# Rounding four weight pieces and preparing chunk 4 ahead of the first join, in an RWKV-7 plus squared-ReLU kernel

## The chip, the cores and the metric

The kernel runs on one core of one Trainium2 chip. The time is the device time of one execution in microseconds (us); the figure given for a kernel is the median of its runs. The core has five engines, each with its own instruction stream, worked off in order: TensorE (PE, matrix products and transposes), VectorE (DVE), ScalarE (ACT), GpSimd (POOL) and SyncE (SP, which here only issues DMAs). An instruction that has to wait holds up everything behind it on its engine.

## The reference

The first half is a recurrence over 768 tokens for 4 batches of 8 heads with head size 40; the second half is a dense layer pair with a squared ReLU on the result, seen as 3072 tokens of 320 numbers.

```python
for t in range(S):
    y[:, :, t] = np.einsum('bhd,bhde->bhe', rt, state)
    Sa = np.einsum('bhde,bhe->bhd', state, at)
    state_decay = state * wt[:, :, None, :] - np.einsum('bhd,bhe->bhde', Sa, bt)
    state = state_decay + np.einsum('bhd,bhe->bhde', vt, kt)
x = y.transpose(0, 2, 1, 3).reshape(B * S, H * D)
h = np.maximum(x @ w_in, 0.0)          # w_in 320 x 2048, w_out 2048 x 320
out = (h * h @ w_out).astype(np.float32)
```

The two weight matrices arrive as 64-bit floats. The kernel reads them as pairs of 32-bit words and makes 32-bit floats of them itself.

## The kernel before

**Chunks and slots.** The tokens are cut into 24 chunks of 128 (6 per batch, the four batches in turn: chunk 0 to 3 are the first of each batch). After a prologue the main loop (L968) runs one *slot* per chunk. Slot i finishes chunk i (`chain`, L604: its first result on ACT is `xr`, L619), makes the parts of chunk i+1 that need no state (`rest` in the first four slots, `sorted_slot` later), and makes `early` parts of later chunks. The dictionary `ahead` says of which: slot 0 makes those of chunks 4 and 5, slot 1 of 6 and 7, slot 2 of 8 and 9, slot 3 of 10, slot 4 of 11 and 12, slot 5 of 13 and 14, and each later slot one.

**The early part of a chunk** (`early`, L342) loads w, b and a (three 160 KB loads on SP), transposes them on PE (L316, three groups of 4), makes running products and reciprocals on DVE (L352, L353, L357, L358, L364, L365), multiplies two of them on PE (L371, listed as L87 `ps_w<-decay,bT`), and copies the result on ACT into the tile `N` (L373 to L377). There is one `N` buffer. From `N` SP stores pieces to DRAM (`kept_q`, `kept_m`, `kept_n`, later `kept_d`), and it stores the decays (`kept_e`). The copy into `N` for the next chunk waits until all stores of the last one have landed. Both `N` and the four PSUM buffers `ps_w` are shared by what the slot does besides.

**Solves and joins.** The triangular systems of a *unit* of chunks (units 0 and 1 are one chunk each, then two chunks each up to chunk 11, then four) are solved on POOL (`solve`, L422 to L453): it fetches `kept_q` into `half_n` (L420), runs 31 pairs of L448 and L450, and stores `kept_t`. The `join` of a chunk (`inverses`, L457) loads `kept_t` as `blocks` (L470), transposes it on DVE (L482) and combines it on PE and ACT (L484, L494, L501) into `T`, which `chain` multiplies with (`xr,T`). Chunk 0's join can't begin before unit 0 is solved.

**Weights.** 26 pieces have to be rounded (`rounding`, L251), two generator steps each; a piece's last instructions come in the next piece's first step. A piece is two ACT instructions (L258, L262) and five DVE ones (L275, L276, L277, L266, L267), with two PSUM buffers `ps_f`. Pieces 0 to 9 (w_in and w_third) are 512 wide, 10 to 25 (w_out) 320 wide. The raw words are fetched in 1 MB fetches (0 to 4, in four or five DMAs) into `wide` buffers and then in 320 KB fetches; `then` (L237) issues a fetch on SP when a piece that held its buffer is done. Fetch 0 is issued by POOL in step 8 of the solve of unit 1, fetch 1 by SP after chunk 0's join, fetch 2 by POOL in step 4 of the solve of unit 2. Slots 0 to 3 round 4, 6, 6 and 7 pieces (`pieces_in`), slot 4 the rest (`halves`).

**The dense layers** (`Ffn`, L689) are woven into the slots from slot 4 on. `thirds` and `whole` need the first ten pieces, `make_quarter` all 26. What is left of them after the last slot runs in `rest` (L760).

The order on each engine is written out: `go`, `run` and `weave` step the generators, `later` and `tick` delay stores and fetches by a step or two.

Of the kernel before, what the change touches and what calls it, by code (L numbers as in the profile page):

```python
# [17 lines left out]
def kernel(  # L18
# [22 lines left out]
    nc = tc.nc  # L41
    ctx.enter_context(tc.manual_schedule())
    B, H, S, D = r.shape
# [72 lines left out]
    class Ring:  # L116
# [6 lines left out]
        def next(self):  # L123
            self.at = (self.at + 1) % len(self.tiles)
            return self.tiles[self.at]
# [10 lines left out]
    order = [(bb, c) for c in range(NCH) for bb in range(B)]  # L136
# [205 lines left out]
    def early(i, g=None, apart=False):  # L342

        x_ = early_loaded.pop(i)
        dec = decays.next() if g is None else kept_here[i]
        if g is not None:
            nc.vector.memset(dec[:, :A_, :, MID:MID + 1], 1.0)
        up, down, aT = (dec[:, n] for n in (UP, DOWN, A_))
        wT = turn(x_["w"])
        yield  # L350
        for q in range(NP):
            nc.vector.tensor_tensor_scan(up[:, q, MID + 1:C + 1], wT[:, q, MID:], ones, 1.0, Alu.mult, Alu.mult)  # L352
            nc.vector.tensor_tensor_scan(down[:, q, MID - 1::-1], wT[:, q, MID - 1::-1], ones, 1.0, Alu.mult, Alu.mult)  # L353
        yield
        if not apart:
            bT_, aT_ = turn(x_["b"]), turn(x_["a"])
        nc.vector.reciprocal(down[:, :, MID + 1:C + 1], up[:, :, MID + 1:C + 1])  # L357
        nc.vector.reciprocal(up[:, :, :MID], down[:, :, :MID])  # L358
        yield
        if apart:  # L360
            bT_, aT_ = turn(x_["b"]), turn(x_["a"])
            yield
        bT = turned("bT", 1)
        nc.vector.tensor_tensor(bT, bT_, down[:, :, 1:C + 1], Alu.mult)  # L364
        nc.vector.tensor_tensor(aT[:, :, :C], aT_, up[:, :, :C], Alu.mult)  # L365
        if g is None:
            store(kept_e[i], dec[:USED])
        yield
        bb, c = order[i]
        t_ = new("N", [128, H, C], 1)  # L370
        for e, p_ in enumerate(products(bT, aT[:, :, :C])):  # L371
            plain, flip_ = t_[:, e:NP:2], t_[:, NP + e::2]
            nc.scalar.copy(plain, p_[:, ::2])  # L373
            for half in range(2):
                own_, other = (slice(n * HC, (n + 1) * HC) for n in (half, 1 - half))
                nc.scalar.copy(flip_[own_, :, own_], p_[other, 1::2, other])  # L376
            nc.scalar.copy(flip_[:HC, :, HC:], p_[:HC, 1::2, HC:])  # L377
        joins = lambda half: t_[half * HC:half * HC + Q, :, half * HC + Q:(half + 1) * HC]
        for half in range(2):
            for n in range(2):  # L380
                at = half * HC + n * Q
                if i < SMALL:
                    kept, to = kept_q[i, :, half, n], at + Q
                else:
                    u = unit_of[i]
                    kept, to = kept_d[u][i - units[u][0], :, half], (half + 1) * HC
                    kept = kept[:, n * Q * HC:n * Q * HC + Q * (to - at)].rearrange("h (s t) -> h s t", s=Q)
                store(kept.rearrange("h s t -> s h t"), t_[at:at + Q, :, at:to], 1, nc.scalar if g is not None and n else nc.sync)
            if i < SMALL and g is None:
                store(kept_m[i][half], joins(half), 1)  # L390
        if g is None:
            store(kept_n[i], t_[:HC, :, HC:], 1)
        else:
            g["dec"], g["N"] = dec, new("N21", [HC, H, HC], 2)
            nc.scalar.copy(g["N"], t_[:HC, :, HC:])
            g["joins"] = spare("joins", i)
            for half in range(2):
                nc.scalar.copy(g["joins"][half * HC:half * HC + Q], joins(half))
        yield
# [11 lines left out]
    def take(u, queues, words=slice(None)):  # L411
        first, nb = units[u]
        if u < FINE:
            kept = kept_q[first:first + nb].rearrange("b h f k s t -> (b h f k) (s t)")
        else:
            kept = kept_d[u].rearrange("b h f w -> (b h f) w")
        cols = classes(u)
        rows = 128 // cols
        for col in range(cols):
            queues[col % len(queues)].dma_start(out=part_of(u)[col * rows:(col + 1) * rows, words], in_=kept[:, words])  # L420

    def solve(u, between={}):  # L422
        run(solving(u, between))
# [177 lines left out]
    halves = (slice(0, HC), slice(HC, C))  # L601
# [170 lines left out]
    second = Ffn()  # L772
# [3 lines left out]
    def run(gen):  # L776
        for _ in gen:
            tick()
# [13 lines left out]
    def prepare(i, g=None, apart=False, steps=0):  # L792
        gen = early(i, g, apart)
        for _ in range(steps):
            next(gen)
            yield
        if i + 1 < len(order) and i + 1 not in early_loaded:
            load_early(i + 1)
        yield from gen
# [6 lines left out]
    ready = {0: {}, 1: {}}  # L806
    own = [nc.gpsimd]
# [5 lines left out]
    def go(gen, n=1):  # L813
        for _ in range(n):
            next(gen, None)
            tick()

    weights = moe_w_in.dtype != FP32
    rounded = rounding() if weights else as_they_are()

    def weights_by(n, queue):
        if weights:
            fetch_weights(n, queue)

    e0, e1, e2, e3 = (early(i, ready[i]) if i in ready else prepare(i) for i in range(B))
    r0, first_slot = rest(0, ready[0]), chain(0, ready[0])
    go(e0, 3)
    go(e1)  # L830
# [25 lines left out]
    flush()  # L856
    join = inverses(0, ready[0])
    go(join)
    go(e3)
    flush()  # L860
    solve(1, {8: lambda: weights_by(0, nc.gpsimd), 20: lambda: take(2, own)})
    run(r0)
    run(join)
    weights_by(1, nc.sync)
    solve(2, {4: lambda: weights_by(2, nc.gpsimd)})
    for gen in (e0, e1, e2, e3):
        run(gen)
    flush()
    tc.no_sync_barrier()


    TOTAL = 12
    ahead = {0: (4, 5), 1: (6, 7), 2: (8, 9), 3: (10,), 4: (11, 12), 5: (13, 14)}
    ahead.update({i: (i + 9,) for i in range(6, len(order) - 9)})

    pieces_in = {0: (4, TOTAL), 1: (6, TOTAL), 2: (6, TOTAL), 3: (7, TOTAL)}
    done = set(range(B))
    unit = unit_of[B]


# [27 lines left out]
    def sorted_slot(i, g, ch):  # L908
        j = i + 1
        more = j < len(order)  # L910
        n = ready.setdefault(j, {}) if more else None
        made = [prepare(m_, apart=True, steps=4 * at) for at, m_ in enumerate(ahead.get(i, ()))]
        one, two = (made + [iter(()), iter(())])[:2]
        early_join = more and "joining" in n
        joining = n.pop("joining") if early_join else inverses(j, n) if more else iter(())
        fine = more and unit_of[j] < FINE

        def step(*what):
            for w_ in what:
                w_()  # L920
            tick()

        of = lambda fn: (lambda: fn(j, n)) if more else (lambda: None)
        on = lambda gen: lambda: next(gen, None)
        begun = i > B

        def extra():
            if not begun:
                second.thirds()
                second.whole()  # L930

        halves = lambda: [next(rounded, None) for _ in range(2)] if not begun else None

        if more:
            begin(j, n)
        step(second.make_quarter, halves, halves)
        step(of(turn_rv), on(one), on(one), halves)
        fetch_next(j + 1, "r")
        step(second.make_quarter, halves)
        step(on(ch), of(decay_state))  # L940
        step(of(make_rv), second.thirds)
        step(on(ch), on(one), on(two), on(two))
        if fine:
            next(joining, None)
        step(second.whole, on(two))
        step(on(ch), extra)
        step(on(one), of(turn_k))
        step(on(one), on(ch), of(turn_down))
        step(on(ch), of(scale_kb))
        if fine:  # L950
            next(joining, None)
        step(on(ch), of(make_a), second.thirds, on(one))
        fetch_next(j + 1, "v")
        step(of(turn_state), second.square, second.whole, on(two), on(two))
        if not early_join:
            next(joining, None)
        step(extra)
        run(ch)
        if more:
            n["chain"] = chain(j, n)  # L960
            next(n["chain"])
        loads(j + 1)
        step(second.square, second.make_quarter)
        step(second.make_quarter, on(two))
        for gen in (one, two, joining):
            run(gen)
# [53 lines left out]
```

## Time and profile before

| | us |
|---|---|
| median of 3 runs | 990.28 (987.42 to 990.52) |
| the profiled execution | 987.0 |
| its span, first to last instruction | 985.3 |
| PE busy in the span | 875.7 (89%) |
| DVE, ACT, POOL busy | 485.0, 275.5, 576.1 |
| `xr` (L619) of chunks 1, 2, 3, 4, 5 | 106.8, 156.1, 204.3, 243.4, 291.8 |

The page gives the busy time of each engine, the span in 40 slices of 24.6 us with the busy share in tenths, the clock that TensorE was granted, and the chain of work that ended last. The timeline gives instructions in order of time: start, duration, engine, line, operation, output and inputs, how many were merged, and in brackets how long the engine had stood idle before and what ended that. "SPq" rows are DMA issues. The `xr` times mark the slots: between the one of chunk i and the one of chunk i+1 lies slot i.

### The profile page before, as it was taken

To read this page: it belongs to the slowest core of one execution; us is meant where nothing else is said; L and a number is where in the kernel's file an instruction comes from. 1 tells how busy PE (TensorE), PEld (TensorE's weight loads), DVE (VectorE), ACT (ScalarE), POOL (GpSimd) and SP (SyncE) were. 2 spreads that over 40 slices of the span, in tenths; PEclk is the share of its full clock that TensorE was granted. 3 is DMA by queue.
4 is the path that set the end of the run, shared out by engine and by line. 5 is a ranking of instruction groups with operands and counts; after the bars stand their busy time and mean duration, and the time that the engine had idled before them with its cause. 6 is when DMAs were issued, how large, how long until landed. Compare 5 with 4: busy or idle time off the path is not lost.

```text
span 985.3 us, 21632 instructions
## 1 busy us (share of the span) xinstructions
PE 875.7 (89%) x8752; PEld 725.8 (74%) x8752; DVE 485.0 (49%) x868; ACT 275.5 (28%) x711; POOL 576.1 (58%) x989
## 2 busy tenths in 40 slices
PE   6447666667897999999999999999999999999998
PEld 4436555556685888888888888888888888887776
DVE  5528775758755454475446655632444423331111
ACT  3132423234323342332223232322222222222111
POOL 4788482836018985999976999959999800000000
PEclk9757565657698999999999999999999999999999
DMA  8987987894667579465588772585404364030000
GB/s 100 143 160 131 191 158 164 171 170 118 91 127 132 100 138 183 92 122 78 97 167 156 124 113 70 102 183 82 66 19 78 82 121 71 14 64 8 14 13 14
DMA packets 263431, 104.16 MB, mean 106 GB/s; under 512 B 246148, under 2 KB 252676, under 8 KB 261924
## 3 DMA queue, kind: packets, MB, share of 16 engines
q1 hardware_dynamic: 259188, 86.39, 50.9%
q0 software_dynamic: 3056, 16.26, 6.9%
q8 instruction: 69, 1.13, 0.5%
q10 hardware_dynamic: 1088, 0.13, 0.1%
q14 instruction: 30, 0.25, 0.1%
HBM read 70.11 MB, written 30.66 MB: 102 GB/s over the span
## 4 chain that ended last, share of the span: by engine, by line
PE 64%; SPq 1%; DVE 1%; DMA 1%; ACT 0%; issue 0%; ACTq 0%
PE ps_f L87 36%; PE ps_w L87 11%; PE ps_c L87 11%; PE ps_w L316 4%; PE ps_c L560 1%; PE ps_c L643 1%; PE ps_w L544 1%; DMA dec<-kept_e 1%; SPq L108 1%; SPq L464 0%; DMA tokens<-tokens 0%; DVE decay L357 0%; DVE state L535 0%; DVE RV L332 0%; ACT N L376 0%
## 5 line engine op out<-in xcount | busy, mean ns | idle before, releaser
L448 POOL TENSOR_TENSOR half_p<-half_n,half_t 128x120 f32<-128x120 f32 (+37 forms) x438 | 255.7, 584 | 84.4 <-DMA half_n<-kept_d 26.5
L450 POOL TENSOR_TENSOR half_t<-half_t,half_p 128x120 f32<-128x120 f32 (+37 forms) x438 | 275.9, 630 | 34.3
L87 PE MATMUL ps_f<-w_out,hid 128*128 128x320 f32 x768 | 217.4, 436 | 0.0
L87 PEld LDWEIGHTS ps_f<-w_out,hid 128*128 128x128 f32 x768 | 142.5, 190 | 54.6 <-issue 0.2
L87 PE MATMUL ps_f<-tokens,w_in 128*128 128x256 f32 x672 | 157.2, 388 | 0.0
L87 PEld LDWEIGHTS ps_f<-tokens,w_in 128*128 128x128 f32 x672 | 126.7, 194 | 17.9 <-issue 1.0
L734 DVE TENSOR_TENSOR hid<-hid 128x512 f32<-128x512 f32 x96 | 88.9, 963 | 50.2 <-ACT hid L727 49.7
L727 ACT ACTIVATE hid<-ps_f 128x512 f32<-128x512 f32 x84 | 50.2, 597 | 96.0 <-PE ps_f L87 96.0
L352 DVE TENSOR_TENSOR_SCAN decay<-ps_w,ones 128x64 f32<-128x64 f32 x88 | 23.8, 271 | 81.5 <-PE ps_w L316 81.5
L669 DVE TENSOR_TENSOR tokens<-ps_c,dec 128x512 f32<-128x512 f32 x24 | 16.5, 688 | 79.3 <-PE ps_c L87 79.3
L87 PE MATMUL ps_w<-decay,bT 40*128 40x128 f32 x352 | 30.0, 308 | 27.0 <-DVE decay L365 27.0
L373 ACT COPY N<-ps_w 128x256 f32<-128x256 f32 x48 | 17.7, 369 | 121.6 <-PE ps_w L87 74.7
L87 PEld LDWEIGHTS ps_w<-decay,bT 40*128 40x128 f32 x352 | 27.6, 213 | 30.2 <-issue 19.1
L510 DVE TENSOR_TENSOR kvT<-ps_w,dec 128x512 f32<-128x512 f32 x24 | 16.5, 688 | 66.9 <-ACT minus_x L630 33.9
L87 PE MATMUL ps_f<-tokens,w_third 64*128 64x256 f32 x336 | 46.9, 385 | 1.5 <-DVE w_out L266 1.5
L332 DVE TENSOR_TENSOR RX<-ps_w,upper 128x512 f32<-128x512 f32 x48 | 30.8, 683 | 32.1 <-PE ps_w L87 31.6
L332 DVE TENSOR_TENSOR RV<-ps_w,upper 128x512 f32<-128x512 f32 x48 | 30.9, 686 | 31.1 <-PE ps_w L87 30.8
L87 PEld LDWEIGHTS ps_c<-xr,T 64*64 64x64 f32 x768 | 30.7, 149 | 20.5 <-issue 15.0
L522 ACT COPY rT<-ps_w 128x512 f32<-128x512 f32 x24 | 14.0, 585 | 108.3 <-PE ps_w L316 108.3
L87 PE MATMUL ps_c<-xr,T 64*64 64x40 f32 x768 | 36.8, 243 | 3.6 <-ACT xr L619 1.6
L357 DVE RECIPROCAL decay<-decay 128x256 f32<-128x256 f32 x22 | 38.2, 1736 | 0.0
L532 DVE TENSOR_TENSOR f<-end,dec 128x4 f32<-128x4 f32 x20 | 5.1, 255 | 66.6 <-DMA dec<-kept_e 66.6
(130 smaller groups left out, 1411.7 us busy)
## 6 DMA issues: line engine op xcount, KB each, us to landing
kept_e<-decay SPq DMA_DIRECT2D x22, 633.8 KB
dec<-kept_e SPq DMA_DIRECT2D x22, 633.8 KB
hid<-in_moe_w_out_dram SPq DMA_DIRECT2D x16, 320.0 KB
half_n<-kept_d POOLq DMA_DIRECT2D x6, 768.0 KB, 10.3
in_w<-in_w_dram SPq DMA_DIRECT2D x24, 160.0 KB
in_ab<-in_b_dram SPq DMA_DIRECT2D x24, 160.0 KB
in_ab<-in_a_dram SPq DMA_DIRECT2D x24, 160.0 KB
in_k<-in_k_dram SPq DMA_DIRECT2D x24, 160.0 KB
```

The lines of the kernel that those rows point to most:

```text
L87: nc.tensor.matmul(o, l_, r_, start=start, stop=True, skip_group_check=True)
L316: nc.tensor.transpose(p_[:, q * 128:(q + 1) * 128], pair(x_, q), ident)
L332: nc.vector.tensor_tensor(t_, p_, over4(upper), Alu.mult)
L352: nc.vector.tensor_tensor_scan(up[:, q, MID + 1:C + 1], wT[:, q, MID:], ones, 1.0, Alu.mult, Alu.mult)
L357: nc.vector.reciprocal(down[:, :, MID + 1:C + 1], up[:, :, MID + 1:C + 1])
L373: nc.scalar.copy(plain, p_[:, ::2])
L448: nc.gpsimd.tensor_tensor(p_, part[:, at:at + m_].unsqueeze(1).to_broadcast([128, n, m_]), t3[:, :n, s:s + 1].to_broadcast([128, n, m_]), ...
L450: nc.gpsimd.tensor_tensor(t3[:, :n, s + 1:], t3[:, :n, s + 1:], p_, Alu.subtract)
L510: nc.vector.tensor_tensor(kT, kT_, down[:, :, 1:C + 1], Alu.mult)
L669: nc.vector.tensor_tensor(t_, y_, g["up"][:, :, :C], Alu.mult)
L727: nc.scalar.activation(h_, p_.rearrange("p f t -> p (f t)"), Act.Relu)
L734: nc.vector.tensor_tensor(h_, h_, h_, Alu.mult)
```

## The change

Fetches 0 and 1 are issued by SP right after the first eight loads. Four pieces are rounded, and chunk 4's early part is begun (four of its five steps), between the DMA issue of chunk 0's join and the rest of that join. Fetch 2 takes fetch 0's place in the solve of unit 1, and the solve of unit 2 issues none. Slots 0 to 3 now round 5, 6, 6 and 6 pieces, slot 4 none; and the early parts are made one chunk further on: slot 0 makes chunk 5's alone, slot 3 those of 10 and 11, slot 4 of 12 and 13, slot 5 chunk 14's alone.

```diff
+    weights_by(0, nc.sync)
+    weights_by(1, nc.sync)
-    e0, e1, e2, e3 = (early(i, ready[i]) if i in ready else prepare(i) for i in range(B))
+    e0, e1, e2, e3, e4 = (early(i, ready[i]) if i in ready else prepare(i) for i in range(B + 1))
...
     join = inverses(0, ready[0])
     go(join)
+    go(rounded, 2 * 4)
     go(e3)
     flush()
-    solve(1, {8: lambda: weights_by(0, nc.gpsimd), 20: lambda: take(2, own)})
+    go(e4, 4)
+    solve(1, {8: lambda: weights_by(2, nc.gpsimd), 20: lambda: take(2, own)})
     run(r0)
     run(join)
-    weights_by(1, nc.sync)
-    solve(2, {4: lambda: weights_by(2, nc.gpsimd)})
-    for gen in (e0, e1, e2, e3):
+    solve(2)
+    for gen in (e0, e1, e2, e3, e4):
         run(gen)
...
-    ahead = {0: (4, 5), 1: (6, 7), 2: (8, 9), 3: (10,), 4: (11, 12), 5: (13, 14)}
-    ahead.update({i: (i + 9,) for i in range(6, len(order) - 9)})
+    ahead = {0: (5,), 1: (6, 7), 2: (8, 9), 3: (10, 11), 4: (12, 13)}
+    ahead.update({i: (i + 9,) for i in range(5, len(order) - 9)})
-    pieces_in = {0: (4, TOTAL), 1: (6, TOTAL), 2: (6, TOTAL), 3: (7, TOTAL)}
-    done = set(range(B))
+    pieces_in = {0: (5, TOTAL), 1: (6, TOTAL), 2: (6, TOTAL), 3: (6, TOTAL)}
+    done = set(range(B + 1))
...
-        halves = lambda: [next(rounded, None) for _ in range(2)] if not begun else None
...
-        step(second.make_quarter, halves, halves)
-        step(of(turn_rv), on(one), on(one), halves)
+        step(second.make_quarter)
+        step(of(turn_rv), on(one), on(one))
         fetch_next(j + 1, "r")
-        step(second.make_quarter, halves)
+        step(second.make_quarter)
```

In the order of instructions that the changed program has, SP issues the eight DMAs of fetches 0 and 1 ahead of chunk 0's first `kept_q` stores. On SP the join's `blocks` load is followed by fetch 3 (five DMAs) and one 320 KB fetch, and only then come the stores of chunk 3's `N`. On PE the products of chunk 4 (`decay,bT`) stand between chunk 0's join and its first `xr,T`; on ACT the copies into `N` for chunk 4 stand between the join's L501 and the chain's first L630.

## The prediction

> **What bounds the kernel now.** I read the slices of the page first: they say when TensorE is the bound.
>
> ```profile
> PE   6447666667897999999999999999999999999998
> PEclk9757565657698999999999999999999999999999
> DMA  8987987894667579465588772585404364030000
> ```
>
> From about 325 us on PE is full at full clock; before 260 us it is half busy at a clock of 0.5 to 0.7 while the DMA engines are near full. So the end is the moment at which PE saturates plus a fixed amount of PE work. A microsecond counts if it moves that moment, or adds to or takes from PE's work after it. The windows by slot show the front part in numbers (columns: window, its length, PE, PE loads, DVE, ACT, POOL busy, clock, DMA share, GB/s):
>
> ```profile
> 62.00:107.00 45.00, 32.95 (x396) 28.89 (x396) 30.07 (x55) 16.52 (x45) 36.92 (x107) 0.61 0.85 152
> 107.00:156.00 49.00, 31.38 (x332) 27.69 (x332) 37.60 (x67) 17.56 (x45) 26.10 (x73) 0.60 0.88 171
> 156.00:204.00 48.00, 30.86 (x334) 26.84 (x332) 32.00 (x67) 16.02 (x45) 24.67 (x68) 0.57 0.84 166
> 204.00:243.00 39.00, 27.74 (x326) 23.76 (x326) 28.93 (x63) 15.04 (x40) 24.83 (x68) 0.63 0.74 141
> ```
>
> These are slots 0 to 3. None is full on any engine. Slots 1 and 2 differ by 5.6 us of DVE work and hardly in length; slot 3, with one early part instead of two, is 9 us shorter. In the timeline, the waits around the change:
>
> ```profile
> 15.22 0.84 SPq L108 DMA_DIRECT2D kept_q<-N  x2
> 19.64 1.16 POOL L420 DMA_DIRECT2D half_n<-kept_q  x2 [9.54 <-DMA kept_q<-N]
> 25.07 0.24 POOL L448 TENSOR_TENSOR half_p<-half_n,half_t 128x31 f32<-128x31 f32 x1 [3.37 <-issue]
> ...
> 49.63 0.61 POOL L453 DMA_DIRECT2D kept_t<-half_t  x1 [0.30 <-POOL half_t L450]
> 50.95 0.37 ACT L373 COPY N<-ps_w 128x256 f32<-128x256 f32 x1 [12.02 <-DMA kept_n<-N]
> 54.34 2.61 SPq L470 DMA_DIRECT2D blocks<-kept_t  x4
> 61.49 0.45 DVE L482 STREAM_TRANSPOSE spares<-blocks 128x256 f32<-128x256 f32 x1 [20.34 <-DMA blocks<-kept_t]
> 67.05 0.60 ACT L630 COPY minus_x<-ps_c 64x160 f32<-64x160 f32 x2 [1.16 <-PE ps_c L87]
> 77.29 0.37 ACT L373 COPY N<-ps_w 128x256 f32<-128x256 f32 x1 [3.08 <-PE ps_w L87]
> 100.72 0.37 ACT L373 COPY N<-ps_w 128x256 f32<-128x256 f32 x1 [8.77 <-DMA kept_n<-N]
> ...
> 284.09 1.95 POOL L420 DMA_DIRECT2D half_n<-kept_d  x4 [41.57 <-DMA kept_d<-N]
> 312.80 1.08 PE L316 MATMUL ps_w<-ident,in_w 128*128 128x128 f32 x4 [5.93 <-DMA in_w<-in_w_dram]
> ```
>
> One serial path leads to the join: `kept_q` stored, `half_n` fetched, 24 us of solve, `kept_t` stored, `blocks` loaded. DVE stands idle 20.34 us for it (41.2 to 61.5). The `N` copies of chunks 3 and 5 wait 12.02 and 8.77 us for the last chunk's stores: the single `N` buffer is the second bound.
>
> **The skill.** "DMA: Bandwidth & Descriptors", section "Queues, rings and completion order", says that each DMA engine takes the descriptors of a ring in order; SP has one row of rings. Trace: the loads behind fetch 1 (SP, 61.4) were issued from 66.6 to 73.7, the third issue alone taking 5.08 us. The same page, "Why a DMA increments its semaphore by 16 and not by 1", says that SP's DMA uses the largest number up to 16 that divides its partitions, on the lowest-numbered engines. For rows 40, 24, 40, 24 that is 10, 12, 10, 12 engines, so ten engines get 12 of a 1 MB fetch's 128 rows (an estimate from the page). The trace's 8 KB packets take about 0.5 us, 6 us a fetch; fetch 3's ran from 99.9 to 107.0, 7.1 us, which agrees. "TensorE: Matmul & The Clock Gate", "What's actually happening", says that the clock halves after an idle window; here it is 0.50 in 40 to 60 us and 0.83 around the 5.93 us wait.
>
> **Part 1, the weights ahead.** The first eight loads' packets end at 11.3. Two fetches keep ten engines busy for 12 us (packets) to 14 us (two times 7.1), to 23.5–25.5. Chunk 0's `kept_q` on SP is behind them. Its stores took from 15.2 to 19.1 before; now their data starts at 24 and lands near 26. SP's `half_n` load waits for it, with b of chunk 0 and all loads of chunks 2 and 3 behind. So unit 0's solve starts about 6.5 us late; bounds are 0 (the DMA engines' idle time from 12 to 16, in which no packet starts, takes up the weights) and 9. I take 6.5: the join moves from 61.5 to 68, and the pre-join DVE work ends near 47.5 instead of 41.2.
>
> **Part 2, the work in the gap.** On DVE four 512-wide pieces, 5 x 0.68 each, issue in about 3.3 us each; the last two instructions come after the join: 12 us. Chunk 4's scans, reciprocals and two products take 6.0 us, as chunk 2's from 29.35 to 35.30. Together 18, from 47.5 to 65.5: hidden in the wait for the join (68). With the cover gone it would cost up to 18. ACT's seven instructions of 0.65 hide likewise.
>
> **Part 3, slot 0.** Behind the join on PE stand chunk 4's products (2.1 us at half clock) and on ACT its `N` copies (2.4 us), ahead of chunk 0's L630. Those copies need the stores of chunk 3's `N`, which on SP now stand behind `blocks` (issued 61 to 63.5), fetch 3 and a 320 KB fetch, while POOL's fetch 2 runs too. 2 MB more take about 12 us: fetch 3 lands near 75, `kept_n` is issued then and lands near 77.5. So the copies run at 78, hardly other than before (77.3), and L630 is at about 80 instead of 67. L630 also releases chunk 5's transposes (PE waits behind `minus_x,N`), so DVE loses its early start as well. From L630, `xr` of chunk 1 came 39.8 us later before. Now chunk 4's products and the 8.8 us wait for `kept_n` go (chunk 4's stores leave at 80 to 86, long ahead of chunk 5's copies); one more 512-wide piece comes (3.3). By engine: RV is done 20.5 us after L630 (21.4 before), PE's next four groups 5, then products, copies, two join steps and `xr`, about 8.5: 34. So chunk 1's `xr` comes at 114: **+7**. Bounds: 0 if part 1 costs nothing, +11.
>
> **Part 4, slots 1 to 3.** Slot 1 rounds one 512-wide piece and five 320-wide ones (2.05 each) instead of six wide: 6.3 us less DVE. A wait for in_w (3.25, PE) limits its first half, so I take **-3** (0 to -6). Slot 2 has two 320 KB fetches fewer: **-1**. Slot 3 gets a second early part and two pieces less. In slot 2 the second chunk's in_w transposition stands ahead of the A products and waits 4.53 us for a load behind k, dec, r, v and b; A came 24.8 us after `xr`, in slot 3 14.9. From A on they took 23.3 and 24.3. With no weight fetches the load comes about 2 us sooner: slot 3 takes 45.5 instead of 39.2, **+6**. Sum at slot 4: +9.
>
> **Part 5, slots 4 and 5.** Slot 4 loses its last rounding (four pieces of 2 us on DVE). PE waited 1.53 us for it (L266 before the first `w_third`), and 4.40 for in_v, which stays: **-1.5**. But POOL's 768 KB fetch for unit 6 (284.1, landed 296.7), which stood in front of slot 5, now comes at slot 4's start, where in_w was used 3.4 us after its issue. 12 us of it beside the other loads delays in_w by 4 to 5 us, with PE at half clock for it: **+5** (0 to 8). Slot 5 makes one early part, not two: PE work 0.60 + 1.04 + 1.16 = 2.8, and the 5.93 us wait for in_w goes, with half of a 6.8 us stretch at half clock (3.4): 12; since the wait may come back in another place, I take **-8** (-2.8 to -12).
>
> **Sum.** +7 -3 -1 +6 -1.5 +5 -8 = +4.5, on a span of 985.3 and an execution of 987.0. The median is 3.3 above that execution, so I set the same 4.5 on the median: 994.8.
>
> **Rivals.** *The weights ride in idle DMA time.* Part 1 costs 1, slot 0 then ends at +2, slot 5 gives its 12, slot 4 no wait: +2 -3 -1 +6 -1.5 -12 = -9.5, 981. For it: DMA idle from 12 to 16 us; 2 MB leave the crowded slots. Against: ring order. It turns on `kept_q` landing before 21. *The stall moves on.* Slot 5 gives only 2.8, and slots 1 and 2 nothing: +7 +6 -1.5 +5 -2.8 = +14, 1004. For it: DMA shares of 0.84 to 0.88. *A wash*: the gains of slot 5 and slot 1 meet the losses within 3 us. That the change does nothing is excluded by the moved instructions; that the gap's work doesn't fit (a join after 72) adds to the second.
>
> **From cases to numbers.** 0.3% (3 us) is about what a measurement of this kernel can tell from none. Slower by 3 to 9 us 0.42, own range 993 to 999; slower by more, 0.20; wash 0.13; faster 0.25. Leaving out a tenth at each end gives 982 to 1004.
>
> **What would show it.** Right: unit 0's first L448 near 31.5, L482 of the join near 68 with under 4 us idle before it, an ACT wait for `kept_n` of 3 us or more before chunk 4's copies, L630 near 80, `xr` of chunk 1 near 114 and of chunk 4 near 252, no wait for in_w in slot 5. Wrong: L448 near 26, or L630 under 73; then slot 0 gains and the sum turns negative. A DVE that reaches the join after its data would show part 2 mispriced.

## The result and the profile after

The changed kernel takes 996.21 us (median of 5 runs, 995.24 to 997.15), beside 990.28 us for the kernel before (median of 5, 986.38 to 992.70). The ratio is 1.0068, with a 95% interval of 1.0040 to 1.0096: slower by 0.7%. The profiled execution took 995.56 us, and its span is 993.9 us, 8.6 longer than before.

The slices of the page, changed kernel (PE's busy share, its granted clock, the DMA engines' share, in fortieths of the span):

```profile
PE   5534785767579999999999999999999999999998
PEclk9855657567589999999999999999999999999999
DMA  9968595986847579375587872594304454030000
```

PE is now full from slice 13 on: the 7 that the kernel before had there (5.93 us of waiting for `in_w`) is gone. But slices 11 and 12 (248 to 298 us), which were 8 and 9, are now 5 and 7, with a clock of 0.5 in slice 11. The windows by slot, from the join to chunk 5 (window, length, PE, PE loads, DVE, ACT, POOL busy, clock, DMA share, GB/s):

```profile
66.00:120.00 54.00, 31.39 (x384) 27.40 (x384) 29.15 (x52) 17.69 (x46) 39.49 (x117) 0.56 0.76 153
120.00:162.00 42.00, 30.64 (x332) 26.98 (x332) 32.91 (x67) 16.28 (x46) 24.68 (x68) 0.62 0.89 168
162.00:211.00 49.00, 30.90 (x332) 26.97 (x332) 31.71 (x67) 16.22 (x46) 24.66 (x68) 0.60 0.81 163
211.00:255.00 44.00, 31.61 (x354) 27.59 (x355) 31.42 (x67) 15.98 (x46) 24.85 (x68) 0.62 0.73 125
255.00:311.00 56.00, 40.57 (x404) 35.00 (x402) 24.02 (x45) 12.72 (x32) 35.62 (x68) 0.79 0.68 116
```

Slot 0 (first line) has less PE and DVE work than before and is 9 us longer from the join on. Slot 1 is 7 us shorter. Slot 4 (last line) is 8 us longer, with less PE work than before (40.57 us; 42.94 in the window from 243 to 292 before). The timeline at the places that the prediction named:

```profile
18.34 1.35 SPq L108 DMA_DIRECT2D kept_q<-N  x2
27.47 1.14 POOL L420 DMA_DIRECT2D half_n<-kept_q  x2 [17.37 <-DMA kept_q<-N]
32.97 0.24 POOL L448 TENSOR_TENSOR half_p<-half_n,half_t 128x31 f32<-128x31 f32 x1 [3.45 <-DMA half_n<-kept_q]
...
60.44 2.61 SPq L470 DMA_DIRECT2D blocks<-kept_t  x4
64.61 0.91 ACT L484 ACTIVATE T<-blocks,which 128x256 f32<-128x256 f32 x2 [4.99 <-DMA blocks<-kept_t]
66.16 0.44 DVE L482 STREAM_TRANSPOSE spares<-blocks 128x256 f32<-128x256 f32 x1
74.90 0.56 SPq L108 DMA_DIRECT2D kept_n<-N  x1
81.12 0.37 ACT L373 COPY N<-ps_w 128x256 f32<-128x256 f32 x1 [10.58 <-DMA kept_n<-N]
83.32 0.60 ACT L630 COPY minus_x<-ps_c 64x160 f32<-64x160 f32 x2
113.88 0.37 ACT L373 COPY N<-ps_w 128x256 f32<-128x256 f32 x1 [1.52 <-issue]
...
258.33 1.95 POOL L420 DMA_DIRECT2D half_n<-kept_d  x4 [8.51 <-DMA kept_d<-N]
259.52 13.76 SPq L470 DMA_DIRECT2D blocks<-kept_t  x2
278.54 1.09 PE L316 MATMUL ps_w<-ident,in_w 128*128 128x128 f32 x4 [10.53 <-DMA in_w<-in_w_dram]
```

The stall at the join has moved, not gone. ACT, and behind it L630 and PE, now wait for chunk 3's `kept_n` (10.58 us). In slot 4 SP needs 13.76 us to issue two loads of `blocks` (4.83 us before), and `in_w`, which stands behind them, comes 10.53 us late for PE. The starts of `xr` (ACT L619) cut the time into slots:

| | chunk 0 | 1 | 2 | 3 | 4 | 5 | 6 |
|---|---|---|---|---|---|---|---|
| before | 30.9 | 106.8 | 156.1 | 204.3 | 243.4 | 291.8 | 337.4 |
| after | 37.3 | 120.0 | 162.0 | 210.8 | 254.7 | 311.4 | 346.8 |
| difference | +6.4 | +13.2 | +5.9 | +6.5 | +11.3 | +19.6 | +9.4 |

From chunk 6 on both kernels run at nearly the same pace (203.7 us to chunk 12 after, 204.8 before, the difference in slot 6; then 343.4 in both to the last `xr`). So what separates the spans, 8.6 us, is made before chunk 6.

### The profile page after: what moved, and what is told of

It reads as the page before. It is cut to its first block, busy times and chain, and to the rows that moved or that the text cites. A ratio compares the mean times of both kernels' runs of the same rounds, so it can differ in the third digit from the quotient of the medians.

```text
span 993.9 us, 21619 instructions
## 1 busy us (share of the span) xinstructions
PE 874.3 (88%) x8752; PEld 724.5 (73%) x8752; DVE 485.2 (49%) x868; ACT 276.2 (28%) x711; POOL 575.3 (58%) x985
## 4 chain that ended last, share of the span: by engine, by line
PE 74%; DVE 8%; DMA 8%; SPq 4%; ACT 3%; issue 2%; ACTq 0%; DVEq 0%
PE ps_f L87 38%; PE ps_w L87 14%; PE ps_c L87 13%; PE ps_w L316 5%; DMA in_w<-in_w_dram 2%; DMA w_out<-in_moe_w_in_dram 2%; SPq L108 1%; PE ps_c L643 1%; SPq L142 1%; DVE decay L357 1%; PE ps_c L560 1%; DMA kept_q<-N 1%; PE ps_w L544 1%; SPq L470 1%; DMA in_k<-in_k_dram 1%
## 5 line engine op out<-in xcount | busy, mean ns | idle before, releaser
L510 DVE TENSOR_TENSOR kvT<-ps_w,dec 128x512 f32<-128x512 f32 x24 | 16.5, 686 | 65.5 <-ACT minus_x L630 35.2
L332 DVE TENSOR_TENSOR RV<-ps_w,upper 128x512 f32<-128x512 f32 x48 | 30.9, 686 | 35.0 <-PE ps_w L87 34.6
L332 DVE TENSOR_TENSOR RX<-ps_w,upper 128x512 f32<-128x512 f32 x48 | 30.9, 685 | 30.2 <-PE ps_w L87 29.7
L532 DVE TENSOR_TENSOR f<-end,dec 128x4 f32<-128x4 f32 x20 | 8.3, 413 | 72.7 <-DMA dec<-kept_e 72.7
L316 PE MATMUL ps_w<-ident,in_ab 128*128 128x128 f32 x192 | 36.1, 346 | 8.6 <-ACT N L377 6.5
L316 PE MATMUL ps_w<-ident,in_w 128*128 128x128 f32 x96 | 20.9, 358 | 21.8 <-DMA in_w<-in_w_dram 17.4
```

Of the source, the lines that this page charges most:

```text
L316: nc.tensor.transpose(p_[:, q * 128:(q + 1) * 128], pair(x_, q), ident)
L332: nc.vector.tensor_tensor(t_, p_, over4(upper), Alu.mult)
L510: nc.vector.tensor_tensor(kT, kT_, down[:, :, 1:C + 1], Alu.mult)
```

## The experiments

Each ratio is to the kernel before, run on the same chip in the same group of runs, with its 95% interval. The changed kernel itself was measured only for the result above. The nearest thing to a repeat is the run with unit 6 behind slot 4, in which no instruction changed its place on its engine: 1.0109. The edits of its group (the first four runs) are best read against that. Two theories run through them. In the first, the three late places (the join, chunk 4's `N` copies, slot 4's `in_w`) are separate delays, each caused by what stands ahead of it in one queue; mend the queue and the time comes back. In the second, the DMA engines are the resource, and an edit that only changes the order lets another transfer be late.

### The weights behind the loads of chunks 2 and 3

```diff
-    weights_by(0, nc.sync)
-    weights_by(1, nc.sync)
...
     load_early(2)
     go(e1)
     flush()
+    weights_by(0, nc.sync)
...
     load_early(3)
+    weights_by(1, nc.sync)
```

> The changed kernel with weight fetch 0 issued on SP behind the first loads of chunk 2 and fetch 1 behind those of chunk 3, instead of both at the top. Theory (part 1 of the prediction: the two fetches stand in SP's ring ahead of chunk 0's kept_q and make unit 0's solve late): unit 0's first L448 at 25 to 26 us instead of 33.0, kept_t issued near 50 instead of 57.6, the join's L482 at 61 to 63 instead of 66.2, now set by DVE's work in the gap; L630 and the end of slot 0 come 3 to 5 us earlier, as the N copies of chunk 4 still wait for chunk 3's stores; about 991 to 993 us. Rival (DVE's gap work or the stores behind it set slot 0, and the weights' place costs nothing): L448 is early but L630 stays at 82 to 84 and xr of chunk 1 at 119 to 121; 995 to 998 us.

996.32 us, ratio 1.0101 [1.0070, 1.0133]. Timeline:

```profile
15.41 0.83 SPq L108 DMA_DIRECT2D kept_q<-N  x2
19.33 0.78 SPq L420 DMA_DIRECT2D half_n<-kept_q  x2
24.74 0.24 POOL L448 TENSOR_TENSOR half_p<-half_n,half_t 128x31 f32<-128x31 f32 x1 [2.91 <-issue]
62.34 5.41 SPq L470 DMA_DIRECT2D blocks<-kept_t  x4
69.56 0.45 DVE L482 STREAM_TRANSPOSE spares<-blocks 128x256 f32<-128x256 f32 x1 [4.27 <-DMA blocks<-kept_t]
80.60 0.37 ACT L373 COPY N<-ps_w 128x256 f32<-128x256 f32 x1 [6.64 <-DMA kept_n<-N]
```

The solve is as early as in the kernel before (24.74), and `kept_t` is issued at 49.34. Still the join comes at 69.56, 3.4 us later than in the changed kernel: SP reached the `blocks` load only at 62.34, because the loads of chunk 1 and the stores of chunk 2 ahead of it had become late (`in_r` and `in_v` took 4.51 and 5.72 us to issue). `xr` of chunk 1 starts at 119.6. Nothing is gained: the 2 MB cost the same at both places ahead of the join. The numbers are those that the rival gave (L630 at 82.80), but not its reason: the place of the weights did cost something, at the join.

### Chunk 3's stores ahead of the next fetches

```diff
-    then = {1: (3,), 2: (WIDE,), 3: (4,), ...
+    then = {3: (4,), ...
...
     go(e3)
     flush()
+    weights_by(3, nc.sync)
+    weights_by(WIDE, nc.sync)
     go(e4, 4)
```

> The changed kernel with fetch 3 and the first 320-wide fetch issued on SP behind chunk 3's N stores instead of ahead of them; the computation and the order on the other engines stay. Theory (part 3: chunk 4's N copies and, behind them on ACT, L630 wait for stores that stand behind these two fetches): kept_n of chunk 3 lands near 70 us instead of 81, N of chunk 4 is copied at 71 to 73, L630 at 73 to 75 instead of 83.3, xr of chunk 1 at 110 to 113 instead of 120.0; about 988 us. Rival (slot 0 is bound by the bytes that the DMA engines carry, so that an earlier L630 meets loads and weights that come 9 us later): xr of chunk 1 at 117 to 121; 994 to 998 us.

999.13 us, ratio 1.0115 [1.0083, 1.0147]. Timeline:

```profile
67.17 0.54 SPq L108 DMA_DIRECT2D kept_n<-N  x1
76.05 0.37 ACT L373 COPY N<-ps_w 128x256 f32<-128x256 f32 x1 [5.78 <-DMA w_out<-in_moe_w_in_dram]
78.25 0.60 ACT L630 COPY minus_x<-ps_c 64x160 f32<-64x160 f32 x2
88.05 1.09 PE L316 MATMUL ps_w<-ident,in_w 128*128 128x128 f32 x4 [8.08 <-DMA in_w<-in_w_dram]
```

`kept_n` was issued 7.7 us earlier, but the copies ran only 5.1 us earlier. The stores now moved beside POOL's fetch 2, issued at 65.26, and the profile puts the end of the copies' wait down to a weight load. L630 came 5.1 us earlier, and PE then waited 8.08 us for chunk 5's `in_w`, which was now issued 4 us behind the two fetches instead of 13. `xr` of chunk 1 starts at 121.9, no earlier than in the changed kernel (120.0) and its repeat (121.5). The second theory holds here.

### Unit 6 behind slot 4 in the program's order

```diff
-        while unit < len(units) and all(...
+        while unit < len(units) and not (unit == 6 and i < B) and all(...
```

> The changed kernel with unit 6's fetch and solve behind slot 4, as in the kernel before, instead of behind slot 3. Theory (part 5: POOL's 768 KB fetch holds up SP's blocks issue, 13.76 us, and in_w behind it, for which PE waits 10.53 us): the blocks issue takes about 5 us, PE's wait for in_w is under 1 us, slot 4 takes 46 to 48 us instead of 56.7, and slot 5 keeps its 35 to 37 us, because no second early part stands there to wait; about 987 us. Rival (the fetch only moves on to slot 5 and delays loads there): slot 4 short, slot 5 at 41 to 46 us with a PE wait for in_k, in_b or in_v; 992 to 996 us.

997.82 us, ratio 1.0109 [1.0089, 1.0129], slot 4 55.7 us. Timeline:

```profile
260.59 1.95 POOL L420 DMA_DIRECT2D half_n<-kept_d  x4 [9.54 <-DMA kept_n<-N]
279.20 1.08 PE L316 MATMUL ps_w<-ident,in_w 128*128 128x128 f32 x4 [9.33 <-DMA in_w<-in_w_dram]
```

Neither expectation was tested, because the edit moved nothing: POOL has no instruction between the two places, so its fetch of `half_n` was issued when chunk 11's stores had landed, 3.7 us after `xr` of chunk 4 (3.6 in the changed kernel). A place in the program moves an instruction in time only if something ahead of it on its engine waits longer. In the two traces every engine has the same instructions in the same order. So this is a second measurement of the changed kernel: it cost 10.9 us here and 5.9 in the first, and `xr` of chunk 1 starts at 121.5.

### The three edits together

```diff
+    weights_by(0, nc.sync)        (behind the loads of chunk 2; fetch 1 behind those of chunk 3)
+    weights_by(3, nc.sync)        (behind chunk 3's stores; then the first 320 KB fetch)
+        ... not (unit == 6 and i < B) ...
```

> The changed kernel with all three edits: weights behind the loads of chunks 2 and 3, chunk 3's stores ahead of the next two fetches, unit 6 behind slot 4. Theory (the three costs are separate places on one path): -4, -8 and -9 add up, less a little that the first two share at the join: 974 to 980 us. Rival (what is won in slot 0 is given back in slots 1 to 3, where DMA is 0.75 to 0.88 busy): xr of chunk 1 early, slots 1 to 3 longer by as much, only slot 4's gain left: 985 to 988 us.

1002.67 us, ratio 1.0144 [1.0109, 1.0178], the slowest of all, though its interval still overlaps that of the repeat (1.0109). The join comes at 71.9, PE waits 10.22 us for chunk 5's `in_w` at 92.0, and `xr` of chunk 1 starts at 125.8. Two edits that each gave nothing give nothing together, and chunk 1 starts 4.2 us later than in the repeat: between 28 and 92 us the transfers were only put in another order, and in each of these traces one that PE needs came last.

### The new dealing alone

```diff
 (kernel before)
-    ahead = {0: (4, 5), 1: (6, 7), 2: (8, 9), 3: (10,), 4: (11, 12), 5: (13, 14)}
+    ahead = {0: (4, 5), 1: (6, 7), 2: (8, 9), 3: (10, 11), 4: (12, 13), 5: (14,)}
...
+        while unit < len(units) and not (unit == 6 and i < B) and all(...
```

> The kernel before with only the dealing of early parts changed: chunks 10 and 11 in slot 3, 12 and 13 in slot 4, 14 alone in slot 5; no weights, pieces or chunk 4 ahead. Theory (slot 5's gain in the changed kernel is the early part that leaves it, and needs nothing of the prologue; slot 3 pays for a second early part): slot 3 longer by 5 to 6 us, slot 5 shorter by 8 to 10, and slot 4 longer by 6 to 9, as in the changed kernel, since unit 6's fetch goes out as soon as chunk 11's stores have landed; 989 to 994 us. Rival (slot 4's loss in the changed kernel comes from its own fewer roundings and another order, not from the fetch): slot 4 within 2 us of the kernel before; 985 to 988 us.

994.45 us, ratio 1.0062 [1.0041, 1.0083]. Timeline:

```profile
258.06 13.07 SPq L470 DMA_DIRECT2D blocks<-kept_t  x2
276.79 1.08 PE L316 MATMUL ps_w<-ident,in_w 128*128 128x128 f32 x4 [7.79 <-DMA in_w<-in_w_dram]
```

Slot 3 took 46.0 us (39.2 before), slot 4 55.8 (48.4), slot 5 35.4 (45.6). So slot 5's gain of 10 and slot 4's loss of 7 both come with the dealing and need nothing of the prologue: the theory is right about these three slots, within a microsecond. The whole time lies just above its range, and in the profile slot 11 takes 3.6 us more than before (36.7 us), of which more below.

### Unit 6's fetch held

```diff
 (changed kernel, with unit 6 behind slot 4)
             flush()
+            if unit == 6:
+                held = single("held", [128, 1])
+                a_ = ready[i + 1]["A"][0][:, 0, :1]
+                nc.gpsimd.tensor_tensor(held, a_, a_, Alu.mult)
+                nc.gpsimd.tensor_tensor(part_of(unit)[:, :1], held, held, Alu.mult)
             take(unit, own)
```

> The changed kernel with unit 6's 768 KB fetch on POOL held until chunk 5's A product is made, late in slot 4, by two POOL instructions of one column that read A and write the fetch's buffer; the rest as it is. Theory (the fetch takes DMA time from SP's loads of slot 4: 13.76 us for the blocks issue, 10.53 us of PE waiting for in_w): the two issues of blocks take about 5 us together, PE waits under 2 us for in_w, slot 4 takes 46 to 50 us instead of 56.7, slot 5 no more than 37; 986 to 990 us. Rival (SP's own queue does it: eight stores of tokens, chunk 11's stores and the loads stand in one ring): blocks and N still take over 10 us to issue, slot 4 over 53 us; 994 to 998 us.

988.39 us (12 runs), ratio 0.9995 [0.9985, 1.0005]. Timeline of slot 4:

```profile
261.24 4.71 SPq L470 DMA_DIRECT2D blocks<-kept_t  x2
271.15 1.09 PE L316 MATMUL ps_w<-ident,in_w 128*128 128x128 f32 x4 [1.48 <-DMA in_w<-in_w_dram]
291.35 1.99 POOL L420 DMA_DIRECT2D half_n<-kept_d  x4 [0.46 <-POOL half_n L991]
```

With the fetch 33 us later the `blocks` issue is back at 4.71 us, the wait for `in_w` at 1.48, slot 4 at 48.8 us; slot 5 keeps its 35.4. SP's own queue has the same work as before the edit, so the rival is out. One transfer of 768 KB at the wrong time was 0.73% of the kernel's time (1.0068 to 0.9995), 7.2 us give or take 3; beside the repeat (1.0109) it is 11 us, and in the profiles slot 4 is 7.9 us shorter. The solve starts 33 us later without harm: the slots after slot 5 are as long as in the changed kernel.

### Chunk 4's products behind the chain

```diff
-    for gen in (e0, e1, e2, e3, e4):
+    for gen in (e0, e1, e2, e3):
...
+        if i == 0:
+            jobs.append((e4, 2, 4, 6))
         jobs.append((rest(i + 1, ready[i + 1]), 9, 2, TOTAL))
```

> The changed kernel with chunk 4's N products, copies and stores moved from ahead of slot 0's chain to behind its second L630; scans, reciprocals and products with b and a stay ahead. Theory (ACT's queue: chunk 4's N copies, waiting 10.58 us for chunk 3's kept_n, hold L630 and the chain behind it): L630 at 70 to 73 us instead of 83.3, chunk 1's xr at 112 to 116 instead of 120.0 with a new PE wait of some 8 us for chunk 5's in_w; 988 to 992 us. Rival (slot 0 is bound by what the DMA engines carry from 60 to 95 us, and the place at which an engine waits for it makes no difference): L630 early, but xr at 118 to 122; 994 to 999 us.

996.39 us, ratio 1.0060 [1.0037, 1.0083]. Timeline:

```profile
71.02 0.60 ACT L630 COPY minus_x<-ps_c 64x160 f32<-64x160 f32 x2 [1.16 <-PE ps_c L87]
79.45 0.66 ACT L262 ACTIVATE w_in<-hid 128x512 f32<-128x512 uint32 x1 [7.14 <-DMA hid<-in_moe_w_in_dram]
82.13 1.09 PE L316 MATMUL ps_w<-ident,in_w 128*128 128x128 f32 x4 [9.39 <-DMA in_w<-in_w_dram]
...
535.75 1.55 PE L87 MATMUL ps_w<-rT,xnT 40*128 40x128 f32 x15 [1.23 <-DVE kvT L510]
```

L630 starts 12.3 us earlier, and of that 3.8 us are left at `xr` of chunk 1 (116.2), between the two expectations. Two other transfers take the place of `kept_n`, and both land at the same time: fetch 2 (79.5), for which the next piece waits on ACT, and chunk 5's `in_w` (82). So three transfers end between 79 and 82 us, and only the first one waited for is seen as a stall. The median gained nothing, but in this profile slot 11 takes 38.5 us instead of 33.1, with PE behind DVE for 1.23 us at 535.8 and a clock of 0.91. The run of the dealing alone has the same there (36.7 us). Two of the five executions took 992.0 and 992.9, the others 996.4 to 997.4; those of the dealing alone are split likewise (992.1 and 993.3, 995.6 and 996.4). That the shorter ones are without the loss in slot 11 would fit, but only one execution of each kernel was profiled, and why those two kernels have it was not tried. So 3.8 us may have been gained and lost again.

### The rounding alone

```diff
 (changed kernel)
-    go(e4, 4)
...
-    ahead = {0: (5,), 1: (6, 7), 2: (8, 9), 3: (10, 11), 4: (12, 13)}
+    ahead = {0: (4, 5), 1: (6, 7), 2: (8, 9), 3: (10,), 4: (11, 12), 5: (13, 14)}
```

> The changed kernel's rounding alone: weight fetches at the top and four pieces ahead of the join, pieces dealt 5, 6, 6, 6, none in slot 4; chunk 4 is made in slot 0 and the early parts are dealt as in the kernel before. Theory (chunk 4's N copies ahead of L630 and the new dealing cost more than they give, the rounding ahead pays): L630 at 70 to 72 us, chunk 1's xr at 112 to 116, slot 1 42 to 46, slot 3 39 to 40, slot 4 46 to 48, slot 5 45 to 46; 986 to 991 us. Rival (the two weight fetches ahead of the join cost slot 0 more than its rounding saves): chunk 1's xr at 117 to 122; 993 to 1000 us.

992.44 us (14 runs), ratio 1.0035 [1.0021, 1.0049]. Timeline:

```profile
70.00 0.60 ACT L630 COPY minus_x<-ps_c 64x160 f32<-64x160 f32 x2 [1.16 <-PE ps_c L87]
79.51 0.67 ACT L262 ACTIVATE w_in<-hid 128x512 f32<-128x512 uint32 x1 [8.22 <-DMA hid<-in_moe_w_in_dram]
80.54 1.38 PE L87 MATMUL ps_c<-xr,T 64*64 64x40 f32 x16 [8.52 <-ACT xr L637]
```

`xr` of chunk 1 starts at 120.7, slot 1 takes 41.9 us, slots 3 to 5 36.7, 48.4 and 46.1. The whole time lies between the two expectations. The rival is right about slot 0: without chunk 4's copies ahead, ACT's instruction for piece 4 waits for fetch 2 and holds L637, and chunk 1 starts no earlier than with them.

### The new dealing, with unit 6's fetch held

> The kernel before with the early parts dealt as in the changed kernel from slot 3 on (10 and 11; 12 and 13; 14) and unit 6's fetch held until chunk 5's A product; no weights, pieces or chunk 4 ahead. Theory (the new dealing is worth slot 5's gain less slot 3's loss once unit 6's fetch doesn't fall into slot 4): slot 3 45 to 46 us, slot 4 47 to 50, slot 5 35 to 36; 985 to 988 us. Rival (the hold only moves the fetch into slot 5, whose loads then wait): slot 5 over 40 us, 990 to 994 us.

984.06 us (18 runs, 981.78 to 986.93), ratio 0.9959 [0.9948, 0.9970]: faster than both kernels, and a microsecond below what the theory gave. The dealing's edit of the kernel before and the two POOL instructions from above are all it takes. Slot 3 took 45.1 us, slot 4 48.8, slot 5 35.4, as the theory says. Windows from chunk 3 to chunk 6:

```profile
207.00:252.00 45.00, 33.04 (x356) 28.58 (x354) 34.93 (x75) 17.49 (x48) 24.85 (x68) 0.58 0.82 159
252.00:301.00 49.00, 43.29 (x416) 37.00 (x414) 30.27 (x62) 15.75 (x39) 6.65 (x20) 0.79 0.68 119
301.00:337.00 36.00, 36.00 (x436) 30.24 (x433) 19.65 (x36) 14.05 (x40) 31.92 (x53) 1.00 0.64 120
```

PE is full at full clock in slot 5 (third line): the early part that stood there has moved to slot 3, where PE is busy for 33 of 45 us.

### Fetch 2 early, and with the new dealing

```diff
 (the rounding alone)
     load(1)
+    weights_by(2, nc.sync)
     go(first_slot)
...
-    solve(1, {8: lambda: weights_by(2, nc.gpsimd), 20: lambda: take(2, own)})
+    solve(1, {20: lambda: take(2, own)})
```

> The run with the rounding alone (chunk 4 not ahead, dealing as before), with fetch 2 issued on SP behind chunk 1's loads, near 43 us, instead of on POOL behind the first join's solve, at 65 us. Theory (slot 0 stalls at 70 to 80 us because piece 4 waits for fetch 2, which moves beside fetch 3 and a 320 KB fetch, and ACT's instruction for it stands ahead of the chain's L637): fetch 2 has landed by 62, no engine waits for it, L637 at 72 to 74 instead of 80.2, chunk 1's xr at 110 to 114 instead of 120.7; 984 to 988 us. Rival (the DMA engines are the bound up to 80 us, and 1 MB earlier only makes chunk 2's and chunk 3's stores and the join late): join at 67 or later, chunk 1's xr at 117 to 122; 991 to 996 us.

> The same with the new dealing from slot 3 on and unit 6's fetch held until chunk 5's A product. Theory (the two edits are separate places): 2 to 4 us below the run with fetch 2 early alone, slot 3 longer by 7 to 9, slot 4 within 2 of it, slot 5 shorter by 10. Rival (without a gain in slot 0 the dealing alone decides): 988 to 992 us.

The first: 989.80 us (16 runs), ratio 1.0010 [0.9998, 1.0022]. Timeline:

```profile
68.05 0.45 DVE L482 STREAM_TRANSPOSE spares<-blocks 128x256 f32<-128x256 f32 x1 [8.28 <-DMA blocks<-kept_t]
75.68 0.60 ACT L637 COPY xr<-ps_c 64x160 f32<-64x160 f32 x2 [0.20 <-PE ps_c L87]
```

L637 starts at 75.7 instead of 80.2, no engine waits for fetch 2 any more, but the join has moved from 64.4 to 68.1 (DVE waits 8.28 us for `blocks`, 4.59 without the edit), and `xr` of chunk 1 starts at 118.1. 2.6 us are gained beside the rounding alone, in the whole time and at chunk 1 alike, where the theory asked for 4.4 at the least, and the rival's late join is there too. The second: 985.41 us (19 runs), ratio 0.9970 [0.9958, 0.9981], 4.4 us below the first, with slot 3 7.7 us longer, slot 4 2.2 longer and slot 5 10.4 shorter, all within half a microsecond of the theory; its rival (988 to 992) is out. So the dealing with the fetch held is worth the same 4 us with the rounding ahead and without it (984.06 beside 988.62), and the rounding ahead adds nothing to it (985.41 beside 984.06).

### The weights from POOL

```diff
-    weights_by(0, nc.sync)
-    weights_by(1, nc.sync)
+    weights_by(0, nc.gpsimd)
+    weights_by(1, nc.gpsimd)
```

> The changed kernel with weight fetches 0 and 1 issued at the top from POOL instead of SP; nothing else moves. Theory (part 1 of the prediction: the delay is order in SP's ring, so chunk 0's kept_q waits only because the 2 MB stand ahead of it there): kept_q on SP is issued near 15.5 us instead of 18.3 and half_n's load by 21, unit 0's first L448 at 26 to 28 us instead of 33.0, in_v without a wait; the join 3 to 5 us earlier than 66.2, limited by DVE's work; 993 to 996 us. Rival (the DMA engines are full with the 2 MB whichever queue they come from, and small stores share them): half_n's load issued at 24 or later, L448 at 30 to 34; 995 to 999 us.

996.38 us, ratio 1.0080 [1.0058, 1.0102]. Timeline:

```profile
10.05 4.18 POOL L249 DMA_DIRECT2D w_out<-in_moe_w_in_dram  x8
15.13 0.83 SPq L108 DMA_DIRECT2D kept_q<-N  x2
25.54 0.78 SPq L420 DMA_DIRECT2D half_n<-kept_q  x2
25.94 1.00 POOL L420 DMA_DIRECT2D half_n<-kept_q  x2 [11.71 <-DMA kept_q<-N]
31.76 0.24 POOL L448 TENSOR_TENSOR half_p<-half_n,half_t 128x31 f32<-128x31 f32 x1 [3.91 <-issue]
```

Now nothing stands ahead of `kept_q` on SP, and it is issued 3.2 us earlier, as in the kernel before (15.22). It lands no earlier than 25 us all the same, against 19 to 20 before. The solve starts at 31.76 instead of 32.97. The join comes 1.7 us earlier (64.50), not 3 to 5. The rival is right: the 2 MB delay the small stores from POOL's queue nearly as much as from SP's own.

## Why the prediction was right, and where it was wrong

**The sum.** Predicted 994.8, measured 996.21. Part of this closeness is luck. The working gave +4.5 on the profiled execution, and the two profiled executions differ by 8.6. The median differs by 5.9 only, because the execution profiled before was 3.3 below its median and the one after 0.65 below; the repeat of the changed kernel cost 10.9. The slots, too, erred both ways: slots 0, 2 and 4 cost 6.2, 1.6 and 4.8 us more than was said, slots 1, 3 and 5 4.3, 1.2 and 2.3 less. Three kernels share their instructions up to slot 3 (the one before and the two dealt anew): chunk 1's `xr` started in them at 106.8, 110.5 and 107.4, so the profile from which all was worked out had one of the shorter slots 0. In the changed kernel and two with the same prologue it started at 120.0, 121.5 and 121.0.

**Part 1 (+6.5 for the first solve): about right in size, wrong in its reason.** Measured 32.97 less 25.07, 7.9; `kept_q` was to land near 26, and `half_n`'s load behind it was issued at 26.95. But the step put it down to the order in SP's ring, the queue in which SP's transfers stand. The run from POOL takes that away and keeps 6.7 of the 7.9. The Trainium skill has the other reason, in "DMA: Bandwidth & Descriptors", section "Issuing engines are not separate DMA queues": transfers from all engines run on the same 16 DMA engines and interleave. The runs agree: from the issue of `kept_q` to that of `half_n`'s load, which waits for it, SP took 10.4 us with the weights in POOL's queue (15.13 to 25.54), and 3.9 us with the weights behind (15.41 to 19.33).

**Part 2 (the gap's work is hidden): nearly.** DVE was to be done at 65.5 and was at 66.2. The data, expected at 68, was there at 64.6: the `blocks` load took 4.2 us from its issue at 60.44, with the DMA engines 0.32 busy. Before it took 7.1 us from its issue at 54.34, with fetch 0 beside it from 56.47 on and the engines 0.59 busy; that this is the cause was not tried apart. So the join is bound by DVE, by 1.5 us, which the prediction had as a sign of a wrong price. The price of DVE's work was right (18.4 us, from 47.75 to 66.16, for 18), that of the load was not.

**Part 3 (slot 0, +7): the path ran as told, with two terms too small, but it is only one of several that end together.** Chunk 4's copies ran at 81.1 instead of 78, L630 at 83.3 instead of 80, and from there to chunk 1's `xr` it took 36.7 instead of 34: 3.3 and 2.7, together 6 of the 6.2 us that are missing. The step named one stall, `kept_n`. Three runs show that this alone does not set slot 0: L630 5.1 us earlier left chunk 1 no earlier, 12.3 us earlier brought it 3.8 us, and with chunk 4 out of the way altogether it started at 120.7. In the changed kernel chunk 3's last store lands at 81 us, and in the runs with the same order of fetches fetch 2 lands at 79.5 and chunk 5's first load at 82, all behind fetch 3 and a 320 KB fetch, with the DMA engines 0.94 busy from 66 to 83. The dependence that I took for the cause was the first of several that end together. In all eleven profiles with fetches 0 and 1 ahead of the join's `blocks` load chunk 1 starts between 116.2 and 125.8, in the three without between 106.8 and 110.6. That the DMA engines are what bounds slot 0 is argued from these: the runs put the same transfers in another order, and none took a fetch out of this stretch without putting it ahead of the join.

**Part 4: slot 1 -7.3 instead of -3, slot 2 +0.6 instead of -1, slot 3 +4.8 instead of +6.** For slot 1 the prediction halved the 6.3 us of DVE work because of a wait for `in_w`; they came in full (41.9 to 43.7 us in every kernel with the pieces ahead, 47.5 to 50.8 in every one without; the means are 6.4 apart). So at chunk 2 the error of slot 0 is nearly made good: +5.9 where +4 was predicted.

**Part 5: slot 4 +8.3 instead of +3.5; slot 5 -10.3 instead of -8.** The place and the cause in slot 4 are right, shown by holding the fetch (8 us back). The term was too small: PE waited 10.53 us for `in_w`, not 4 to 5, because SP's issue of `blocks` itself was held, 13.76 us instead of 4.7, with `in_w` behind it. The prediction priced the loads beside the fetch, not the issue that it holds up. The -1.5 for the rounding that leaves slot 4 does not show clearly: with the dealing as before slot 4 took 48.4 and 46.8 us without the rounding and 48.4 with it, with the new dealing and the fetch held 48.8 and 48.9 without and 48.8 with it. Slot 5 gave most of the 12 that were counted, and the wait did not come back in another place.

**The rivals.** Weights riding in idle DMA time: false, it turned on `kept_q` landing before 21. The stall moving on, at 1004: half of it, in slot 0 and slot 4, but slots 1 and 5 gave more than it allowed.

**What the parts are worth.** By the ratios, in us of 988.6: the rounding ahead alone +3.5; the new dealing with the fetch held -4.1; both with chunk 4 ahead and the fetch held -0.5, which leaves +0.1 for chunk 4; the fetch in slot 4 +7.2. Together +6.7, the change, as they must, since two of the four are differences. The intervals are one to three us wide on each side; with the repeat (1.0109) in place of the first measurement the fetch is +11 and the change +10.8. That chunk 4's part costs nothing is a remainder: it was not measured alone.

## What to carry to other kernels

Before you move a large transfer, list every transfer that runs beside it and who waits for each. In slot 0, with the DMA engines 0.76 to 0.94 busy, another queue or another place ahead of the same wait only moved the stall. The stall of slot 4 went away when the fetch was held to a stretch in which PE waited for no load. When a stall names one transfer, look for others that land within a few microseconds of it before you price its removal. And when work is made earlier, ask what its results set off: here the data of unit 6 were ready one slot sooner, and the fetch that went out by itself cost more (7 to 11 us) than the new dealing gives (4 us).

## What the runs showed of the hardware that was not expected

- Four stores of 32 KB each, two issued by SP and two by ACT, while 2 MB of loads from POOL's queue were in flight, took some 10 us to land (15.13 to 25.5), against 4 us without them.
- An issue on SP can be held by traffic of another queue: two `blocks` loads took 13.76 us to issue beside POOL's 768 KB and 4.71 us without. What SP issued next was late by the same: `in_w` went out 15.6 us after the start of the `blocks` issue (275.11) instead of 6.5 (267.77 in the run with the fetch held).
- The same instructions, run in three kernels up to slot 3, differed by 3.7 us at chunk 1's `xr`, where whole executions of the kernel before lay between 984.57 and 992.93 in one group of 47. In this crowded stretch a slot's length read from one profile is no better than that.
